# One triangle of symmetric attention scores computed, the other taken by DMA transpose, with a PSUM ring of double banks and chunked loads, in a gated attention and MLP-mixer kernel

## The chip, the cores and the metric

The kernel runs on one core of one Trainium2 chip. The metric is the device time of one execution in microseconds; the runs of a kernel are summarised by their median.

## What is computed

Eight batches of 3008 rows. `z` has 64 columns; `u` and `v` have 256. First a gated attention without softmax, then an MLP mixer over tokens and over channels, with the attention's output as its input:

```python
scores = (z @ z.T) / S                      # per batch, S = 3008: symmetric
attn = np.maximum(scores, 0.0) ** 2
x = u * (attn @ v)
# mixer
h = np.maximum(x.T @ w_tok1, 0.0) @ w_tok2  # w_tok1 3008x256, w_tok2 256x3008
u2 = x + h.T
out = u2 + np.maximum(u2 @ w_ch1, 0.0) @ w_ch2   # w_ch1 256x1536, w_ch2 1536x256
```

Inputs and output are float32; the kernel works in bf16 with float32 sums.

## The kernel before

Rows are handled in 24 tiles of 128 (the last has 64 real rows). Queries are taken in 6 blocks of 512 (the last 448 wide), keys in 6 groups of 4 tiles, so a batch has 36 groups (b, q, g): query block q against key group g. The loop runs over all 288 groups of the 8 batches.

*Attention.* `load_z` (line 67) loads z twice side by side with a casting DMA on POOL's queue, so that it fills 128 columns, and one DMA transpose on SP's queue makes `zT` (line 80): both halves of the partitions hold z transposed. `scores` (line 134) makes the scores of a group with four 64-row matmuls (line 145), two of them in the upper and two in the lower half of the rows of the array, into two PSUM tiles `sc` of two banks each; ACT applies relu and 1/S (line 151, `rl`), DVE squares (line 153, `at`). The result has keys on partitions and queries along the row. `av` (line 157) multiplies it by `v`: per key tile two matmuls of 512 columns (line 177), one for each half of v's 256 columns, both into `acc`, one PSUM tile of two banks for the whole query block. The last key tile has only 64 rows; its copy on the other 64 partitions serves the second half. After the sixth key group `gate` (line 183) multiplies `acc` by the transposed `u` (lines 191 and 196 on DVE) into `xT`, and a DMA transpose makes `x` (line 199). The `acc` tag has one buffer, so the next query block's first matmul waits for the gate. `load_uT` (line 96) loads a u block and transposes it (line 108).

*Mixer.* `mixer(b)` (line 214) returns pieces of work that are run between the attention matmuls of batch b+1: `tok1` (line 226: 8 matmuls of 256 columns into `a_ps`, over the six query blocks one sum), `tok2` (line 239: `h_ps`, added to `xT` by DVE on line 243), `ch1` (line 257: `hp`, one bank, 512 channels-by-rows per piece, relu on ACT, line 209, or DVE, line 212, whichever a running count has less loaded) and `ch2` (line 271: 24 matmuls of 256 columns into `op`; the sum with `u_sb` on DVE, line 277, and the store, line 281). All mixer tiles share the tag `mm`: two single banks. PSUM is so divided: two `sc` tiles of two banks, `acc` two banks, `mm` two banks.

*Order.* The program is emitted by hand and every engine's queue keeps that order. In group n the scores of group n+1 come first, then the four key tiles of group n, and after each of them mixer pieces as long as a budget lasts; a batch's share of mixer cost is spread evenly over the 36 groups. Each piece has an earliest group. In batch 0 no mixer work exists; after the last group the whole mixer of batch 7 is left and runs alone. At the very start (lines 312 to 316) POOL's queue gets z, v, u block 0, all weights and u block 1 of batch 0, in this order; the next batch's z is fetched at its query block 1 and its v at block 2.

Of the kernel before, what the change touches and what calls it, by code (L numbers as in the profile page):

```python
# [7 lines left out]
F32 = mybir.dt.float32  # L8
# [4 lines left out]
P = 128  # L13
QW = 512
# [13 lines left out]
def kernel(  # L28
# [38 lines left out]
    def load_z(b):  # L67


        zr = sb.tile([P, KT, 2, d_qk], BF16, tag="zr", name="zr", bufs=1)  # L70
        for h in range(2):
            nc.gpsimd.dma_start(
                out=zr[:, : KT - 1, h, :],
                in_=z[b, : (KT - 1) * P, :].rearrange("(t p) d -> p t d", p=P))
            for r in range(2):
                nc.gpsimd.dma_start(
                    out=zr[r * TAIL:(r + 1) * TAIL, KT - 1, h, :],
                    in_=z[b, (KT - 1) * P:, :])
        zT = sb.tile([P, KT, P], BF16, tag="zT", name="zT", bufs=2)
        nc.sync.dma_start_transpose(out=zT[:], in_=zr.rearrange("p t h d -> p (t h d)"))  # L80
        return zT.rearrange("p t s -> p (t s)")

    def load_v(b, parts):
        vt = sb.tile([P, KT, D], BF16, tag="v", name="v_sb", bufs=2)
        step = (KT - 1 + parts - 1) // parts
        for t0 in range(0, KT - 1, step):
            t1 = min(t0 + step, KT - 1)
            nc.gpsimd.dma_start(  # L88
                out=vt[:, t0:t1, :],
                in_=v[b, t0 * P:t1 * P, :].rearrange("(t p) d -> p t d", p=P))  # L90
        for r in range(2):
            nc.gpsimd.dma_start(
                out=vt[r * TAIL:(r + 1) * TAIL, KT - 1, :], in_=v[b, (KT - 1) * P:, :])
        return vt

    def load_uT(b, q):
        ur = sb.tile([P, QW // P, D], BF16, tag="ur", name="ur", bufs=2)
        full = widths[q] // P
        rest = widths[q] - full * P
# [11 lines left out]
        return uT  # L111
# [16 lines left out]
    zTs, vs, uTs = {}, {}, {}  # L128
    xTs, xs = {}, {}
    groups = [(b, q, g) for b in range(B) for q in range(NQ) for g in range(NG)]  # L130
    accs = {}
    attn = {}

    def scores(n):
        b, q, g = groups[n]
        zT = zTs[b]
        W = widths[q]
        tiles = []
        pss = []
        for pr in range(GK // 2):  # L140
            sc = psum.tile([P, 2, QW], F32, tag="sc", name="sc", bufs=2)
# [7 lines left out]
        for sc in pss:  # L149
            rl = sb.tile([P, 2, QW], BF16, tag="rl", name="rl", bufs=3)  # L150
            nc.scalar.activation(rl[:, :, :W], sc[:, :, :W], ACT.Relu, scale=inv_S)  # L151
            at = sb.tile([P, 2, QW], BF16, tag="at", name="at", bufs=5)
            nc.vector.tensor_mul(at[:, :, :W], rl[:, :, :W], rl[:, :, :W])  # L153
            tiles.append(at)
        attn[n] = tiles

    def av(n):

        b, q, g = groups[n]
        W = widths[q]  # L160
        if g == 0:
            accs[b, q] = psum.tile([P, DT, QW], F32, tag="acc", name="acc", bufs=1)
        acc = accs[b, q]
        tiles = attn.pop(n)
        vt = vs[b]
        order = list(range(GK))
        if g == NG - 1:
            order = [GK - 1] + order[:-1]

        def one(i, last):  # L170
            k = g * GK + i
            at = tiles[i // 2][:, i % 2, :W]
            for dh in range(DT):
                rows = slice(0, P)
                if k == KT - 1:
                    rows = slice(dh * TAIL, (dh + 1) * TAIL)
                nc.tensor.matmul(  # L177
                    acc[:, dh, :W], vt[rows, k, dh * P:(dh + 1) * P], at[rows],
                    start=(k == 0), stop=(g == NG - 1 and last), skip_group_check=True)

        return [lambda i=i, j=j: one(i, j == GK - 1) for j, i in enumerate(order)]

    def gate(b, q):
        W = widths[q]
        acc = accs.pop((b, q))
        uT = uTs.pop((b, q))
        xT = sb.tile([P, DT, QW], BF16, tag="xT", name="xT", bufs=13)
        if W < QW:
            nc.gpsimd.memset(xT[:, :, W:], 0.0)
        full, rest = W // P, W % P  # L190
        nc.vector.tensor_mul(  # L191
            xT[:, :, :full * P].rearrange("p h (t s) -> p h t s", s=P),
            acc[:, :, :full * P].rearrange("p h (t s) -> p h t s", s=P),
            uT[:, :full].rearrange("p t h s -> p h t s"))
        if rest:
            nc.vector.tensor_mul(
                xT[:, :, full * P:W], acc[:, :, full * P:W], uT[:, full, :, :rest])
        x = sb.tile([P, DT, QW // P, P], BF16, tag="x", name="x_sb", bufs=7)
        nc.sync.dma_start_transpose(
            out=x.rearrange("p h t d -> p (h t) d"), in_=xT.rearrange("p h s -> p (h s)"))  # L200
        xTs[b, q], xs[b, q] = xT, x


    load = {"ACT": 0.0, "DVE": 0.0}

    def relu_out(dst, src, n):
        if load["ACT"] + 0.1 + n / 1200 <= load["DVE"] + 0.15 + n / 960:
            load["ACT"] += 0.1 + n / 1200
            nc.scalar.activation(dst, src, ACT.Relu)  # L209
        else:  # L210
            load["DVE"] += 0.15 + n / 960
            nc.vector.tensor_single_scalar(dst, src, 0.0, AX.max)  # L212

# [174 lines left out]
```

## Time and profile before

| | |
|---|---|
| median of 3 runs | 1467.13 us (1466.74 to 1468.72) |
| the profiled execution | 1467.17 us |
| span of its profile (first to last instruction) | 1465.4 us |
| PE busy | 1296.3 us, 7488 matmuls |
| DVE / ACT busy | 700.0 / 760.6 us |
| DMA | 105.75 MB, mean 72 GB/s |

The profile takes one execution apart by engine: PE is the matrix engine (PEld its weight loads), DVE and ACT the two elementwise engines, POOL and SP the queues that here issue DMAs. A row "A <- B" under waits says that A's engine stood idle until B was done, with the total, the number of times and the longest, all in us. A row of the timeline starts with its time from the start of the span and its length. In a row of instruction groups stand the count, the busy time, the mean in ns, and the idle time before. A matmul's end is modelled, so its duration overlaps with the next one's; start-to-start distances are what counts.

### The profile page before, as it was taken

The page shows a single profiled execution, that of the slowest core. Times are in us where ns is not written, and L with a number is a line of the kernel's source. Part 1 is how long each engine was busy: PE and PEld are TensorE (multiplying, and loading weights), DVE is VectorE, ACT ScalarE, POOL GpSimd, SP SyncE. Part 2 cuts the span into 40 slices and gives each one's busy share as a digit, 9 for nine tenths or more (in the row PEclk, how much of TensorE's full clock was granted, in tenths as well). Part 3 has the DMA queues.
Part 4 walks back from the last instruction along what each step waited for, and adds up shares of the span by engine and source line. Part 5 has one row for each costly group of instructions (what it writes and reads, how often), then busy time and mean ns, then how long its engine had stood idle before and what let it go on. Part 6 is the DMA issues. An engine that isn't in the chain of part 4 may idle for free.

```text
span 1465.4 us, 18578 instructions
## 1 busy us (share of the span) xinstructions
PE 1296.3 (88%) x7488; PEld 630.6 (43%) x7488; DVE 700.0 (48%) x1028; ACT 760.6 (52%) x965; POOL 126.9 (9%) x178
## 2 busy tenths in 40 slices
PE   1998889998999889988999989989899898999987
PEld 0334344543445334443444434445344453444455
DVE  0565554454544544445444454444544445454432
ACT  1776455545655455554555445554555544555232
POOL 5221000110010100100001100011000000000000
PEclk9999999999999999999999999999999999999999
DMA  9997522663234732629225482155512223111311
GB/s 160 174 130 87 93 46 56 73 100 71 51 62 68 121 64 45 72 50 130 54 45 65 72 125 47 43 62 97 99 43 44 58 49 72 36 37 30 70 37 49
DMA packets 308070, 105.75 MB, mean 72 GB/s; under 512 B 230224, under 2 KB 307472, under 8 KB 307984
## 3 DMA queue, kind: packets, MB, share of 16 engines
q1 hardware_dynamic: 202624, 68.71, 23.0%
q0 software_dynamic: 105360, 35.86, 22.6%
q8 instruction: 58, 0.95, 0.3%
q14 instruction: 28, 0.23, 0.0%
HBM read 71.70 MB, written 24.64 MB: 66 GB/s over the span
## 4 chain that ended last, share of the span: by engine, by line
PE 60%; ACT 13%; DVE 11%; issue 10%; DMA 5%; POOL 0%; ACTq 0%; DVEq 0%; SPq 0%; POOLq 0%
PE acc L177 22%; PE op L271 18%; PE hp L257 11%; ACT rl L151 9%; PE sc L145 6%; ACT h2pre L209 4%; DVE xT L191 3%; DMA x_sb<-xT 3%; DVE at L153 3%; DVE h2pre L212 2%; DVE xT L243 2%; PE h_ps L239 2%; PE a_ps L226 1%; DMA zT<-zr 1%; DVE res L277 0%
## 5 line engine op out<-in xcount | busy, mean ns | idle before, releaser
L151 ACT ACTIVATE rl<-sc 128x1024 bf16<-128x1024 f32 (+1 forms) x576 | 547.9, 1003 | 488.6 <-PE sc L145 487.8
L177 PE MATMUL acc<-at,v_sb 128*128 128x512 bf16 (+2 forms) x2304 | 593.0, 376 | 52.5 <-DVE xT L191 38.6
L153 DVE TENSOR_TENSOR at<-rl 128x1024 bf16<-128x1024 bf16 (+1 forms) x576 | 391.6, 681 | 462.9 <-ACT rl L151 461.9
L257 PE MATMUL hp<-xT,w_ch_sb 128*128 128x512 bf16 (+1 forms) x1152 | 318.7, 374 | 56.6 <-ACT h2pre L209 40.2
L177 PEld LDWEIGHTS <-v_sb 128*128 128x128 bf16 (+1 forms) x2304 | 203.3, 97 | 337.3 <-issue 162.6
L209 ACT ACTIVATE h2pre<-hp 128x512 bf16<-128x512 f32 (+1 forms) x380 | 217.7, 592 | 155.9 <-PE hp L257 154.3
L271 PE MATMUL op<-w_ch_sb,h2pre 128*128 128x256 bf16 (+1 forms) x2304 | 267.7, 273 | 13.5 <-ACT h2pre L209 12.0
L271 PEld LDWEIGHTS <-h2pre 128*128 128x128 bf16 (+1 forms) x2304 | 225.6, 98 | 64.0 <-issue 23.6
L257 PEld LDWEIGHTS <-w_ch_sb 128*128 128x128 bf16 x1152 | 109.4, 97 | 222.6 <-issue 122.9
L145 PE MATMUL sc<-zT 64*128 64x512 bf16 (+1 forms) x1152 | 173.9, 378 | 30.1 <-DMA zT<-zr 28.8
L212 DVE TENSOR_SCALAR h2pre<-hp 128x512 bf16<-128x512 f32 (+1 forms) x196 | 132.7, 679 | 112.2 <-PE hp L257 111.5
L277 DVE TENSOR_TENSOR res<-op,u_sb 128x512 f32<-128x512 f32 x88 | 60.9, 692 | 161.6 <-PE op L271 161.6
L100 POOL DMA_DIRECT2D ur<-in_u_dram x48 | 36.6, 763 | 991.8 <-DMA uT<-ur 919.0
L145 PEld LDWEIGHTS <-zT 64*128 64x128 bf16 x1152 | 36.3, 94 | 150.4 <-issue 121.6
L243 DVE TENSOR_TENSOR xT<-xT,h_ps 128x512 bf16<-128x512 bf16 (+1 forms) x96 | 61.1, 674 | 9.2 <-PE h_ps L239 6.9
L239 PE MATMUL h_ps<-w_tok_sb,a_sb 128*128 128x512 bf16 (+1 forms) x192 | 54.1, 373 | 10.4 <-DVE xT L243 9.1
L191 DVE TENSOR_TENSOR xT<-acc,uT 128x1024 bf16<-128x1024 f32 (+1 forms) x48 | 56.5, 1176 | 7.4 <-PE acc L177 7.4
L226 PE MATMUL a_ps<-x_sb,w_tok_sb 128*128 128x256 bf16 x384 | 45.7, 272 | 2.2 <-DMA x_sb<-xT 2.1
L226 PEld LDWEIGHTS <-w_tok_sb 128*128 128x128 bf16 x384 | 37.5, 98 | 12.4 <-issue 4.1
L239 PEld LDWEIGHTS <-a_sb 128*128 128x128 bf16 x192 | 18.4, 96 | 44.1 <-issue 29.4
L88 POOL DMA_DIRECT2D v_sb<-in_v_dram x32 | 27.0, 861 | 93.2 <-PE acc L177 93.2
L232 ACT ACTIVATE a_sb<-a_ps 128x512 bf16<-128x512 f32 x8 | 4.8, 597 | 47.5 <-PE a_ps L226 47.5
(19 smaller groups left out, 74.8 us busy)
## 6 DMA issues: line engine op xcount, KB each, us to landing
out_dram<-res SPq DMA_DIRECT2D x88, 256.0 KB, 2.1
ur<-in_u_dram POOLq DMA_DIRECT2D x40, 256.0 KB, 4.2
v_sb<-in_v_dram POOLq DMA_DIRECT2D x24, 384.0 KB, 8.1
zr<-in_z_dram POOLq DMA_DIRECT2D x16, 368.0 KB, 7.0
v_sb<-in_v_dram POOLq DMA_DIRECT2D x8, 320.0 KB, 12.1
w_ch_sb<-in_moe_w_ch_dram POOLq DMA_DIRECT2D x2, 768.0 KB, 27.6
ur<-in_u_dram POOLq DMA_DIRECT2D x8, 192.0 KB, 3.6
w_tok_sb<-in_moe_w_tok_dram POOLq DMA_DIRECT2D x1, 1504.0 KB, 26.5
```

What stands on the lines that cost most here:

```text
L145: nc.tensor.matmul(sc[:, r, :W], zT[h, k * P:(k + 1) * P], zT[h, q * QW:q * QW + W], start=True, stop=True)
L151: nc.scalar.activation(rl[:, :, :W], sc[:, :, :W], ACT.Relu, scale=inv_S)
L153: nc.vector.tensor_mul(at[:, :, :W], rl[:, :, :W], rl[:, :, :W])
L177: nc.tensor.matmul(acc[:, dh, :W], vt[rows, k, dh * P:(dh + 1) * P], at[rows], start=(k == 0), stop=(g == NG - 1 and last), skip_group_che ...
L191: nc.vector.tensor_mul(xT[:, :, :full * P].rearrange("p h (t s) -> p h t s", s=P), acc[:, :, :full * P].rearrange("p h (t s) -> p h t s", ...
L209: nc.scalar.activation(dst, src, ACT.Relu)
L212: nc.vector.tensor_single_scalar(dst, src, 0.0, AX.max)
L226: nc.tensor.matmul(st["a_ps"][:, th, :], w_tok1_sb[:, k, th * P:(th + 1) * P], x[:, :, i, :], start=(k == 0 and th == 0), stop=(k == KT - ...
L239: nc.tensor.matmul(h[:, :W], st["a"][:, th, dh * P:(dh + 1) * P], w_tok2_sb[:, th, q * QW:q * QW + W], start=(th == 0), stop=(th == 1))
L243: nc.vector.tensor_add(xT[:, dh, :W], xT[:, dh, :W], h[:, :W])
L257: nc.tensor.matmul(hp[:, :W], w_ch1_sb[:, dc, cc * P:(cc + 1) * P], xTs[b, q][:, dc, :W], start=(dc == 0), stop=(dc == DT - 1))
L271: nc.tensor.matmul(op[:rows[i], i, :], h2[:, cc, c0:c0 + rows[i]], w_ch2_sb[:, cc, :], start=(cc == 0 and i == 0), stop=(cc == CHT - 1), s ...
```

## The change

*Scores.* Only groups with g >= q are computed ("direct", 21 of 36 per batch). For g > q the squares are written to `at` in blocks of 128x128, and a DMA transpose on SP's queue makes `fl` from it (16 blocks): the tile that group (q'=g, g'=q) needs later. `fl` has ten buffers, `at` three, each for a whole group. The order of key groups in a query block now mixes direct and flipped ones.

*PSUM.* One tag `ps` of three double banks serves scores and all mixer pieces; `tok2` and `ch1` make two 512-column results per tile and one DVE or ACT instruction reads both, by strict turns for `ch1`. `acc` is split in two single-bank tiles, one for each half of the columns of v; in a group all matmuls of one half come first, then the other's, and the gate runs by halves between them.

*Loads.* z and v are loaded in chunks of one key group (z through two buffers, each chunk with its own transpose), at the start and for the next batch.

*Pace.* The budget follows the estimated length of each group; mixer pieces are run between and after the two halves of a group.

```diff
-    def load_z(b):
-        zr = sb.tile([P, KT, 2, d_qk], BF16, tag="zr", name="zr", bufs=1)
+    def load_z(b, zT, c):
+        t0, t1 = c * GK, min(c * GK + GK, KT - 1)
+        zr = sb.tile([P, GK, 2, d_qk], BF16, tag="zr", name="zr", bufs=2)
...
+        nc.sync.dma_start_transpose(
+            out=zT[:, t0:t0 + GK, :], in_=zr.rearrange("p t h d -> p (t h d)"))
...
+    def load_v(b, c):
+        vt = sb.tile([P, GK, D], BF16, tag="v", name="v_sb", bufs=8)
...
+    def key_order(q):
+        direct = list(range(q, NG))
+        if q == 0:
+            return [direct[0], direct[-1]] + direct[1:-1]
+        direct = [direct[-1]] + direct[:-1]
+        flipped = list(range(q))
+        order = []
+        while direct or flipped:
+            if direct:
+                order.append(direct.pop(0))
+            if flipped:
+                order.append(flipped.pop(0))
+        return order
+
+    groups = [(b, q, g) for b in range(B) for q in range(NQ) for g in key_order(q)]
+    directs = [t for t in groups if t[2] >= t[1]]
...
-            sc = psum.tile([P, 2, QW], F32, tag="sc", name="sc", bufs=2)
+            sc = psum.tile([P, 2, QW], F32, tag="ps", name="sc", bufs=3)
...
-            at = sb.tile([P, 2, QW], BF16, tag="at", name="at", bufs=5)
-            nc.vector.tensor_mul(at[:, :, :W], rl[:, :, :W], rl[:, :, :W])
+        at = sb.tile([P, GK * QW], BF16, tag="at", name="at", bufs=3)
+        flip = g > q
...
+            if flip:
+                r4 = rl.rearrange("p i (j s) -> p j i s", s=P)
+                nc.vector.tensor_mul(a4[:, :, pair, :], r4, r4)
+            else:
+                nc.vector.tensor_mul(a3[:, pair, :W], rl[:, :, :W], rl[:, :, :W])
+        if flip:
+            attn[b, q, g] = a4.rearrange("p j i s -> p i j s")
+            fl = sb.tile([P, GK, QW], BF16, tag="fl", name="fl", bufs=10)
+            nc.sync.dma_start_transpose(
+                out=fl.rearrange("p j (i s) -> p (j i) s", s=P), in_=at[:])
+            attn[b, g, q] = fl[:, :, :]
...
-            accs[b, q] = psum.tile([P, DT, QW], F32, tag="acc", name="acc", bufs=1)
+            accs[b, q] = [
+                psum.tile([P, QW], F32, tag=f"acc{h}", name=f"acc{h}", bufs=1)
+                for h in range(DT)]
...
-    def gate(b, q):
+    def gate(b, q, dh):
...
-        def tok2(q, dh):
-            h = psum.tile([P, QW], F32, tag="mm", name="h_ps", bufs=2)
+        def tok2(q):
+            h = psum.tile([P, DT, QW], F32, tag="ps", name="h_ps", bufs=3)
...
-            nc.vector.tensor_add(xT[:, dh, :W], xT[:, dh, :W], h[:, :W])
+            nc.vector.tensor_add(xT[:, :, :W], xT[:, :, :W], h[:, :, :W])
...
-            hp = psum.tile([P, QW], F32, tag="mm", name="hp", bufs=2)
+            hp = psum.tile([P, 2, QW], F32, tag="ps", name="hp", bufs=3)
...
-            relu_out(st["h2", q][:, cc, :W], hp[:, :W], W)
+            turn[0] += 1
+            if turn[0] % 2:
+                nc.vector.tensor_single_scalar(h2[:, :, :W], hp[:, :, :W], 0.0, AX.max)
+            else:
+                nc.scalar.activation(h2[:, :, :W], hp[:, :, :W], ACT.Relu)
...
+    load_z(0, zTs[0], 0)
+    load_v(0, 0)
+    for c in vorder[1:]:
+        load_z(0, zTs[0], c)
+        load_v(0, c)
+    load_uT(0, 0)
+    load_weights()
+    load_uT(0, 1)
...
+        if not last:
+            half(0)
+            mix(n, got / 2)
+            half(1)
+            mix(n, 0.0)
+        else:
+            half(0)
+            gate(b, q, 0)
+            half(1)
+            gate(b, q, 1)
+            mix(n, 0.0)
```

What the change moves on SP's queue: its first instructions before, all of them DMA transposes (`zT` of batch 0, three u blocks, `x` of query block 0, `zT` of batch 1; the numbers tell tiles apart):

```order
L80 DMA_TRANSPOSE zT_77<-zr_70 128x24x128
L108 DMA_TRANSPOSE uT_88<-ur_86 128x8x128
L108 DMA_TRANSPOSE uT_98<-ur_96 128x8x128
L108 DMA_TRANSPOSE uT_161<-ur_159 128x8x128
L199 DMA_TRANSPOSE x_sb_253<-xT_251 128x8x128
L80 DMA_TRANSPOSE zT_262<-zr_255 128x24x128
```

The same place after it, from the fifth z chunk of batch 0 on:

```order
L82 DMA_TRANSPOSE zT_70<-zr_99 128x4x128
L82 DMA_TRANSPOSE zT_70<-zr_105 128x4x128
L108 DMA_TRANSPOSE uT_113<-ur_111 128x8x128
L108 DMA_TRANSPOSE uT_123<-ur_121 128x8x128
L182 DMA_TRANSPOSE fl_151<-at_144 128x16x128
L182 DMA_TRANSPOSE fl_176<-at_169 128x16x128
L108 DMA_TRANSPOSE uT_188<-ur_186 128x8x128
L182 DMA_TRANSPOSE fl_203<-at_196 128x16x128
L182 DMA_TRANSPOSE fl_226<-at_219 128x16x128
L182 DMA_TRANSPOSE fl_249<-at_242 128x16x128
L182 DMA_TRANSPOSE fl_272<-at_265 128x16x128
```

The first flips (`fl`) stand behind the transposes of u blocks 0 and 1 and, after two of them, u block 2; on POOL's queue the load of u block 1 (`ur_121`) still stands behind the weights.

DVE's queue at the start of the last mixer, before (`h_ps` and `hp` are single banks of PSUM):

```order
L243 TENSOR_TENSOR xT_11966<-xT_11966,h_ps_12296 128x512
L243 TENSOR_TENSOR xT_11966<-xT_11966,h_ps_12300 128x512
L243 TENSOR_TENSOR xT_12199<-xT_12199,h_ps_12306 128x448
L243 TENSOR_TENSOR xT_12199<-xT_12199,h_ps_12310 128x448
L212 TENSOR_SCALAR h2pre_12316<-hp_12333 128x512
L212 TENSOR_SCALAR h2pre_12316<-hp_12341 128x512
```

and after (double banks):

```order
L284 TENSOR_TENSOR xT_10339<-xT_10339,h_ps_10598 128x1024
L284 TENSOR_TENSOR xT_10494<-xT_10494,h_ps_10604 128x2x448
L306 TENSOR_SCALAR h2pre_10612<-hp_10613 128x1024
L306 TENSOR_SCALAR h2pre_10626<-hp_10627 128x1024
L306 TENSOR_SCALAR h2pre_10640<-hp_10641 128x1024
L327 TENSOR_TENSOR res_10679<-op_10654,u_sb_10610 128x512
```

One instruction stands where two stood; `ch1` of a block is read by three of them on DVE (and three on ACT), and `ch2`'s first sum follows.

More of the change, by code (lines that the diff above doesn't have):

```diff
@@ L75, in load_z @@
             for r in range(2):
                 nc.gpsimd.dma_start(
[L77 to L94, printed above, removed]
+                    out=zr[r * TAIL:(r + 1) * TAIL, GK - 1],
@@ new lines, in both_tails, with half @@
+        def both_tails():
+            for dh in range(DT):
+                mm(GK - 1, dh, first, False)
+        def half(dh):
+            n = GK - 1 if tail else GK
+            for i in range(n):
+                mm(i, dh, first and i == 0 and not tail, last and i == n - 1)
+        pre = [both_tails] if tail else []
+        return pre, half
+    def gate(b, q, dh):
+        W = widths[q]
+        acc = accs[b, q][dh]
+        uT = uTs[b, q]
+        if dh == 0:
+            xTs[b, q] = sb.tile([P, DT, QW], BF16, tag="xT", name="xT", bufs=9)
+            if W < QW:
+                nc.gpsimd.memset(xTs[b, q][:, :, W:], 0.0)
+        xT = xTs[b, q]
@@ L198, in gate @@
[L198 to L212, printed above, removed]
```

282 lines of the change are left out of this document (153 added, 129 removed).

## The prediction

> **What bounds the kernel now.** I began with the page's first part and the stretches of the span, to see whether one engine is full all the way.
>
> ```profile
> PE 1296.3 (88%) x7488; PEld 630.6 (43%) x7488; DVE 700.0 (48%) x1028; ACT 760.6 (52%) x965; POOL 126.9 (9%) x178
> 0.00:40.00 40.00, 10.26 (x44) 3.26 (x44) 5.22 (x8) 8.93 (x9) 19.66 (x28) 1.00 1.30 165
> 520.00:690.00 170.00, 154.10 (x901) 75.84 (x900) 83.23 (x123) 88.81 (x113) 14.68 (x21) 1.00 0.44 66
> 1365.00:1465.40 100.40, 84.53 (x520) 50.07 (x518) 34.95 (x54) 27.26 (x48) 0.00 (x0) 0.99 0.20 52
> ```
>
> The last three rows are 40 us at the start, 170 us of the middle and the last 100 us: length, then the busy time of PE, PEld, DVE, ACT and POOL, PE's clock, DMA share, GB/s. PE is the engine that matters: about nine tenths busy in the middle at full clock, while DVE and ACT are half busy and the DMA engines stand at 0.44. At the start PE works 10 of 40 us.
>
> Next, who PE waits for (total, times, longest):
>
> ```profile
> PE hp L257 <- ACT h2pre L209: 40.2, 94, 0.9
> PE acc L177 <- DVE xT L191: 38.6, 40, 1.2
> PE sc L145 <- DMA zT<-zr: 28.8, 1, 28.8
> PE op L271 <- ACT h2pre L209: 12.0, 21, 0.7
> PE hp L257 <- DVE h2pre L212: 11.6, 38, 0.4
> PE acc L177 <- DVE xT L196: 10.4, 7, 1.5
> PE h_ps L239 <- DVE xT L243: 9.1, 33, 0.5
> ```
>
> Apart from one wait for the first transposed z, all are short waits for a PSUM tile to be read: the gate after each query block, and the single banks of the mixer.
>
> Then PE's pitch, because its busy time is modelled and overlaps. Three rows of PE in batch 0, where no mixer runs, and the mean durations by form:
>
> ```profile
> 55.17 0.60 PE L145 MATMUL sc<-zT 64*128 64x512 bf16 x4
> 55.70 1.90 PE L177 MATMUL acc<-at,v_sb 128*128 128x512 bf16 x8
> 57.54 0.60 PE L145 MATMUL sc<-zT 64*128 64x512 bf16 x4
> 706.78 2.78 PE L271 MATMUL op<-w_ch_sb,h2pre 128*128 128x256 bf16 x24
> L177 PE MATMUL acc<-at,v_sb 128*128 128x512 bf16 x1840 | 489.1, 380 | 42.3 <-DVE xT L191 31.9 <-DVE xT L196 10.4
> L271 PE MATMUL op<-w_ch_sb,h2pre 128*128 128x256 bf16 x2208 | 256.3, 272 | 13.5 <-ACT h2pre L209 12.0 <-DVE h2pre L212 1.5
> ```
>
> Eight 512-column matmuls take 1.90 us with one's tail of 0.38: pitch 0.217 us, eight are 1.74. A 256-column one: (2.78 - 0.27)/23 = 0.109. A group is 57.54 - 55.17 = 2.37, so its four score matmuls cost 0.63.
>
> Last, the ends of batch 0 and batch 7, from the transposes that follow the gates:
>
> ```profile
> 124.88 1.60 SPq L199 DMA_TRANSPOSE x_sb<-xT  x1
> 1369.26 1.28 SPq L199 DMA_TRANSPOSE x_sb<-xT  x1
> ```
>
> The span is thus 124.9 (start and batch 0), 7 batches of (1369.3 - 124.9)/7 = 177.8, and a tail of 96.1 in which the last mixer runs alone. Pure pitch of one middle batch: acc 276 full-width equivalents (288, less the 448-wide block and the paired tail rows), h_ps 23.5 and hp 141, all at 0.217: 95.6; a_ps 48 and op 288 at 0.109: 36.6; 36 score bursts at 0.63: 22.7. Sum 154.9. The other 23 us per batch are the waits above, each with the 0.16 of the next matmul's start that the modelled tail hides.
>
> **The change, part by part.** *Scores.* 21 of 36 groups keep their burst: 15 x 0.63 = 9.5 us less per batch, so the pitch floor is 145.4. Relu and multiply go with them, off PE's path.
>
> *The flips.* 15 per batch, 16 blocks of 128x128 each. Rows for transposes of 8 and 24 blocks (SP's issue time min/median/max, the landing, and the 16 engines in 3.4 us around one 8-block transpose):
>
> ```profile
> L108 SPq DMA_TRANSPOSE uT<-ur x48: 1232/1282/5532, 24.1 to 1294.5; - x48
> L80 SPq DMA_TRANSPOSE zT<-zr x8: 3612/3731/9844, 10.1 to 1037.2; - x8
> uT<-ur SPq DMA_TRANSPOSE x48, 3.1
> zT<-zr SPq DMA_TRANSPOSE x8, 5.7
> q1 hardware_dynamic: 1056, 0.26, 40.0%
> ```
>
> Sixteen blocks: issue 3.73 x 16/24 = 2.5 us, landing between 3.1 and 5.7, say 4.4; DMA engines 2 x 0.40 x 3.4 = 2.7 us. Per batch that is 37 us of SP and 41 us of DMA on top of 0.44 x 170 = 75: 116 of some 155. Every flipped tile is produced at least six groups (10 us or more) before its use, so landing is hidden in the steady state. The cover is thin only in block 0 of each batch: five flips, one each 2.37 us, almost no mixer work beside them, three `at` buffers. SP needs 2.5 each. Cost 0 to 6 us per batch (the upper end if each is 1.2 us late, as an 8-block transpose has landed after up to 13.5), I take 2.
>
> ```profile
> DMA to landing us min/median/max: 3.0/3.2/13.5
> ```
>
> The Trainium skill speaks against these flips: its page "VectorE: DVE Perf Modes", section "The three transpose paths", prices one 128x128 transpose at 390 ns on TensorE and 1309 ns by DMA, and advises TensorE where the result may go to PSUM. In the rows above the 24 blocks of zT land in 5.7 us together, 0.24 us a block, so the page's figure is not one that adds up over blocks; the sum by it stands among the rivals.
>
> *The loads in chunks.* They are more DMAs on POOL's queue, which is 9% busy. A v chunk waits until PE has done with the chunk before in the last block, and is used seven groups (12 us or more) later; the nearest row, half as large again, lands in 8.1: hidden.
>
> ```profile
> v_sb<-in_v_dram POOLq DMA_DIRECT2D x24, 384.0 KB, 8.1
> ```
>
> *The flipped multiply.* It writes in runs of 128. Bounds from the nearest rows: 0.69 as the contiguous bf16 one (L153), 1.22 as a PSUM one of the same size (L191); I take 0.69, the same types and count.
>
> ```profile
> L153 DVE TENSOR_TENSOR at<-rl 128x1024 bf16<-128x1024 bf16 x480 | 331.5, 692 | 387.9 <-ACT rl L151 387.0
> L191 DVE TENSOR_TENSOR xT<-acc,uT 128x1024 bf16<-128x1024 f32 x40 | 48.8, 1221 | 5.3 <-PE acc L177 5.3
> L151 ACT ACTIVATE rl<-sc 128x1024 bf16<-128x1024 f32 x480 | 465.1, 1021 | 404.7 <-PE sc L145 404.5
> L212 DVE TENSOR_SCALAR h2pre<-hp 128x512 bf16<-128x512 f32 x165 | 113.4, 689 | 101.4 <-PE hp L257 100.9
> ```
>
> At 1.22 DVE would get 16 us more per batch, on an engine that is half idle. The same page of the Trainium skill, section "What auto-detection actually checks", asks only for 16-bit tensors of step one, by which it would stay at 0.69.
>
> *Double banks.* An hp pair is 4 x 0.217 = 0.87 us of PE; its eviction is 1.02 on ACT (L151) or 1.22 on DVE (L191's size), by turns, so each engine has 1.74. With three slots a slot is wanted two pairs, 1.74 us, after it is full, and free 1.22 and some 0.2 of signalling (an estimate) after: no wait where DVE and ACT have nothing else. In the 21 direct groups two multiplies (1.38) or two relus (2.04) stand ahead of it in their queue: 0 to 0.5 us each, 0 to 10 per batch; I take 4. The six tok2 adds are all on DVE in one burst: 6 x 1.22 = 7.3 against 5.2 of PE, 0 to 2.1; 2. The first ch2 of a block wants the last pair 10 matmuls (1.1 us) after its end, which is ready 1.2 to 1.4 after: 6 x 0.15 to 0.4, I take 1.
>
> *Gate by halves.* A half is 0.69 (512 columns from PSUM, as L212) and starts while PE does the other half (0.87); the next block's scores or mixer work cover the second. The tail rows of key block 5, first in blocks 1 to 5, want both: 0 to 0.4 six times; 1. Uncovered, the whole was 49 us in 47 waits.
>
> So a batch has 145.4 + 2 + 4 + 2 + 1 + 1 = 155.4. The bounds add to 146 and 168; a batch at either end in every term is unlikely, so 148 to 165 goes into the range. Seven: 1088.
>
> *Start and batch 0.* PE can begin as soon as one z chunk is loaded and transposed, near 9 us (issue from 1.2, and at most the 4.2 and 3.1 of a whole u block) instead of 28.8. But SP's queue is in order, and the flips stand behind the transposes of u blocks 0 and 1, whose second loads behind the weights:
>
> ```profile
> 12.13 1.50 POOL L115 DMA_DIRECT2D w_tok_sb<-in_moe_w_tok_dram  x1
> 22.61 0.76 POOL L100 DMA_DIRECT2D ur<-in_u_dram  x1
> 24.15 1.30 SPq L108 DMA_TRANSPOSE uT<-ur  x1
> 51.18 5.48 SPq L108 DMA_TRANSPOSE uT<-ur  x2
> ur<-in_u_dram POOLq DMA_DIRECT2D x40, 256.0 KB, 4.2
> ```
>
> In before that u block landed at 51.2, and nobody minded. Now PE does four groups by about 22 us and stops: the multiply of the fifth needs the `at` buffer of the first flip. The new z loads pass through two buffers, so the third to sixth each wait for a load and a transpose, some 7 us, two in flight at a time: the sixth is issued near 9 + 1.5 x 7 = 20, and the weights behind it near 23 instead of 12, while less is queued ahead of them. I put that landing at 54 (45 to 62). Then: transpose of u 1.3, first flip landed at 60, and SP is the bound until it has issued the nine flips of blocks 0 and 1 (22.5) and some 6 us of other transposes: 84, where PE stands at block 2. Remaining: 10 x 2.37 + 14 x 1.74 = 48. Batch 0 ends near 133 (122 to 145) against 124.9: the early start is worth nothing and costs 8.
>
> *Tail.*
>
> ```profile
> 1374.75 8.02 DVE L243 TENSOR_TENSOR xT<-xT,h_ps 128x512 bf16<-128x512 bf16 x12 [5.64 <-PE h_ps L239]
> 1382.22 3.75 PE L257 MATMUL hp<-xT,w_ch_sb 128*128 128x512 bf16 x12
> ```
>
> The adds shrink from 8.0 to 7.3. From 1382.2 to the end is 83.2 us, 3.7 of them after PE's last op; PE's work there is 6 x (6 x 0.87 + 48 x 0.109) = 62.7, less 0.6 for the narrow block, plus 6 x 0.3: 64 instead of 79.5. Tail 96.1 - 16 = 80 (77 to 84).
>
> *Sum.* 133 + 1088 + 80 = 1301 of span; the profiled execution was 1467.17 for a span of 1465.4, so 1.8 more: 1303. That execution is within 0.1 us of the median of the runs, 1467.13.
>
> **The rivals.** *Slower: the DMA engines become the bound.* A batch gets longer than 177.8 once a flip costs (177.8 - 75)/15 = 6.9 us of all engines. For it: while the weights load, two 8-block issues took 5.48 us, 5.5 for sixteen blocks, and the first zT 9.84, 6.6 for sixteen. Against: alone it is 2.7, and later medians are near the minima. At 8 us: 75 + 120 = 195 per batch, 145 + 7 x 195 + 80 = 1590. I give it 0.05. *Slower: blocks one after another at a fixed price.* 240 blocks per batch decide against the change from (177.8 - 75)/240 = 0.43 us a block. At the slowest issue of the rows, 5.53/8 = 0.69, a batch is 75 + 166 = 241 and the sum 145 + 7 x 241 + 82 = 1914. Against it: 0.24 a block with landing, 0.16 of issue. 0.01. By the 1309 ns of the Trainium skill's page "VectorE: DVE Perf Modes", section "The three transpose paths", it would be 75 + 314 per batch and some 2950 in all; the landing of zT disagrees.
>
> *The waits only move.* One ring for everything lets a slow read block scores and mixer alike, and the multiply that waits for a flip blocks evictions behind it on DVE. At 26 us of waits per batch, more than the 23 of before: 133 + 7 x 171.4 + 84 + 2 = 1419. For it: DVE and ACT do shared work in order; against: both half idle. 0.12 for 1380 to 1464.
>
> *Better.* Waits of 3 and batch 0 ending at 115: 115 + 7 x 148.4 + 78 + 2 = 1234. 0.07 for below 1245.
>
> *Nothing changes.* PE's queue has 14018 rows instead of 14978, 480 matmuls fewer with their weights, so the work does go; only waits that exactly replace it give no change: 0.01.
>
> **How the numbers follow.** The forecast, 0.74, gives 1303. Its bounds: 122 + 7 x 148.4 + 77 + 2 = 1240 and 145 + 7 x 165 + 84 + 2 = 1386; not all ends meet, so 1245 to 1380, which leaves out the rivals on both sides. Faster by over 0.2% (about what a measurement of this kernel can tell from no change): 0.74 + 0.12 + 0.07 = 0.93; within 0.2%: 0.01; slower: 0.06.
>
> **What would show it.** Right: PE idle from about 22 to 60 us, ended through DVE's multiply by the first flips, which stand on SP behind uT; batch 0 ends after 125; batches of 148 to 165; gate waits nearly gone; flip issue near 2.5 us. Wrong: DMA share near 1 in the middle, SP issues of 5 us there, PE waits over 20 us per batch for hp, sc or h_ps, or a PE that runs through the first 60 us.

## The result, and the profile after

The changed kernel takes 1268.69 us in the median of 4 runs (1266.92 to 1276.55), against 1466.93 us for the kernel before in 4 runs on the same chip (1465.94 to 1468.72): a ratio of 0.866, 95% interval 0.862 to 0.870. The profiled execution took 1268.15 us for a span of 1266.4. The forecast was 1303 in a range of 1245 to 1380.

The first row is the one that the prediction began with, busy time and share of the engines from the page:

```profile
PE 1185.9 (94%) x6929; PEld 623.5 (49%) x7008; DVE 578.1 (46%) x744; ACT 472.2 (37%) x489; POOL 174.7 (14%) x258
```

Then 151 us of the middle (start:end, length; busy PE, PEld, DVE, ACT, POOL; PE's clock; DMA share; GB/s):

```profile
433.00:584.00 151.00, 148.74 (x886) 79.44 (x894) 72.23 (x93) 58.77 (x61) 21.94 (x32) 1.00 0.90 139
```

PE is idle for 2.3 of 151 us there. DVE and ACT do less, and the DMA share has gone from 0.44 to 0.90. Next, who PE and the flipped multiply wait for in the whole execution (total, times, longest):

```profile
DVE at L176 <- DMA fl<-at: 57.0, 7, 39.2
PE acc L212 <- DVE at L176: 32.6, 10, 27.7
PE sc L159 <- DMA zT<-zr: 21.7, 6, 9.4
PE acc L212 <- DVE xT L238: 12.2, 20, 1.9
PE h_ps L280 <- ACT a_sb L272: 0.7, 1, 0.7
PE hp L301 <- ACT h2pre L308: 0.2, 1, 0.2
```

The mixer's waits (`hp`, `op`, `h_ps`: 73 us before) are gone, and the gate's are 12.2 instead of 49. What is left is in batch 0: the transposes of z, and the multiply (line 176) that waits for a flip to give its `at` buffer back. The last transposes of batches 0 and 7, from SP's timeline, mark their ends as before:

```profile
145.32 3.59 SPq L247 DMA_TRANSPOSE x_sb<-xT  x1
1185.84 1.23 SPq L247 DMA_TRANSPOSE x_sb<-xT  x1
```

The flip's line on SP (issue in ns, min/median/max) and its landing in us:

```profile
L182 SPq DMA_TRANSPOSE fl<-at x120: 1317/2116/6943, 59.1 to 1140.7; - x120
DMA to landing us min/median/max: 4.2/4.8/11.6
```

So the span is 145.3 + 7 x 148.6 + 80.6. Against before, batch 0 ends 20.4 us later, each of the seven batches is 29.1 shorter (-203.9 in all), and the tail is 15.5 shorter: -199.0.

The loss sits in the first 70 us. PE there, first its start and then the stop, SP's transposes, and what SP itself waited for longest in the first 150 us:

```profile
9.39 1.03 PE L159 MATMUL sc<-zT 64*128 64x512 bf16 x4 [9.39 <-DMA zT<-zr]
35.79 1.04 PE L159 MATMUL sc<-zT 64*128 64x512 bf16 x4 [5.18 <-DMA zT<-zr]
64.54 3.57 PE L212 MATMUL acc<-at,v_sb 128*128 128x512 bf16 x8 [27.71 <-DVE at L176]
30.30 28.74 SPq L108 DMA_TRANSPOSE uT<-ur  x2
59.14 4.41 SPq L182 DMA_TRANSPOSE fl<-at  x2
SPq L108 <- DMA ur<-in_u_dram: 37.8, 3, 26.2
```

PE starts at 9.4 instead of 28.8, does four groups, and stands for 27.7 us until the first flips have landed. These stood on SP behind two u transposes. The merged row from 30 to 59 is not two slow transposes: SP was done with the first by 31.6, and then stood 26.2 us for the load of u block 1. The weights were issued on POOL from 25.3 to 29.8 us and that load right behind them; the channel weights took 26.1 to land, the u block about 28.

### The profile page after: what moved, and what is told of

The parts are those of the page before. It is cut to its first block, busy times and chain, and to the rows that moved or that the text cites. A ratio compares the mean times of both kernels' runs of the same rounds, so it can differ in the third digit from the quotient of the medians.

```text
span 1266.4 us, 17085 instructions
## 1 busy us (share of the span) xinstructions
PE 1185.9 (94%) x6929; PEld 623.5 (49%) x7008; DVE 578.1 (46%) x744; ACT 472.2 (37%) x489; POOL 174.7 (14%) x258
## 4 chain that ended last, share of the span: by engine, by line
PE 80%; DMA 7%; DVE 6%; issue 3%; ACT 2%; POOL 1%; SPq 0%; DVEq 0%; ACTq 0%; POOLq 0%
PE acc L212 34%; PE op L319 20%; PE hp L301 17%; PE sc L159 5%; DMA fl<-at 4%; PE a_ps L266 3%; DVE xT L284 3%; DMA ur<-in_u_dram 2%; ACT rl L172 2%; DVE h2pre L306 1%; DVE at L176 1%; DVE xT L238 1%; DMA zr<-in_z_dram 1%; DMA zT<-zr 0%; PE h_ps L280 0%
## 5 line engine op out<-in xcount | busy, mean ns | idle before, releaser
L172 ACT ACTIVATE rl<-sc 128x1024 bf16<-128x1024 f32 x336 | 324.2, 1016 | 451.8 <-PE sc L159 422.5
L212 PE MATMUL acc<-at,v_sb 128*128 128x512 bf16 (+1 forms) x1337 | 337.5, 385 | 45.3 <-DVE at L176 32.6
L176 DVE TENSOR_TENSOR at<-rl 128x1024 bf16<-128x1024 bf16 x240 | 165.5, 692 | 271.7 <-ACT rl L172 206.6
L308 ACT ACTIVATE h2pre<-hp 128x1024 bf16<-128x1024 f32 (+1 forms) x144 | 144.9, 1006 | 281.6 <-PE hp L301 263.9
L212 PE MATMUL acc<-fl,v_sb 128*128 128x512 bf16 (+1 forms) x921 | 223.8, 370 | 2.2 <-issue 0.2
L306 DVE TENSOR_SCALAR h2pre<-hp 128x1024 bf16<-128x1024 f32 (+1 forms) x144 | 172.6, 1200 | 79.6 <-PE hp L301 79.5
L73 POOL DMA_DIRECT2D zr<-in_z_dram x96 | 72.3, 759 | 454.9 <-DMA zT<-zr 453.6
L159 PE MATMUL sc<-zT 64*128 64x512 bf16 (+1 forms) x672 | 105.4, 385 | 23.8 <-DMA zT<-zr 21.7
L178 DVE TENSOR_TENSOR at<-rl 128x1024 bf16<-128x1024 bf16 (+1 forms) x96 | 64.3, 680 | 76.5 <-ACT rl L172 71.1
L238 DVE TENSOR_TENSOR xT<-acc,uT 128x512 bf16<-128x512 f32 (+1 forms) x96 | 61.8, 665 | 71.7 <-PE acc L212 71.2
## 6 DMA issues: line engine op xcount, KB each, us to landing
w_ch_sb<-in_moe_w_ch_dram POOLq DMA_DIRECT2D x2, 768.0 KB, 26.1
```

Source lines behind the costliest of these rows:

```text
L73: nc.gpsimd.dma_start(out=zr[:, : t1 - t0, h, :], in_=z[b, t0 * P:t1 * P, :].rearrange("(t p) d -> p t d", p=P))
L159: nc.tensor.matmul(sc[:, r, :W], zT[h, k * P:(k + 1) * P], zT[h, q * QW:q * QW + W], start=True, stop=True)
L176: nc.vector.tensor_mul(a4[:, :, pair, :], r4, r4)
L212: nc.tensor.matmul(o, vt[rows, i, dh * P:(dh + 1) * P], rhs, start=st, stop=sp, skip_group_check=True)
L238: nc.vector.tensor_mul(xT[:, dh, :full * P].rearrange("p (t s) -> p t s", s=P), acc[:, :full * P].rearrange("p (t s) -> p t s", s=P), uT[: ...
L306: nc.vector.tensor_single_scalar(h2[:, :, :W], hp[:, :, :W], 0.0, AX.max)
```

## The experiments

Line numbers in the rows of an experiment are those of its own kernel. All are compared with the changed kernel (ratio 0.866 to before); "batch" is the usual distance of two batches' ends. The four runs of the changed kernel spread over 9.6 us, so a smaller difference of medians is read together with the batch ends, which come from the one profiled execution of each kernel.

| run | median, us | ratio to before (95%) | batch 0 ends | batch |
|---|---|---|---|---|
| changed kernel | 1268.69 | 0.866 (0.862 to 0.870) | 145.3 | 148.9 |
| u blocks ahead of the weights | 1279.62 | 0.871 (0.869 to 0.873) | 157.8 | 148.9 |
| weights spread over groups 8 to 22 | 1288.40 | 0.877 (0.873 to 0.882) | 162.7 | 148.9 |
| nothing flipped | 1335.84 | 0.910 (0.909 to 0.912) | 126.6 | 161.3 |
| six raw z buffers | 1282.0 | 0.873 (0.872 to 0.875) | 148.1 | 148.9 to 153.0 |
| no ring | 1375.72 | 0.937 (0.936 to 0.939) | 144.5 | 161.3 |
| gate whole | 1269.46 | 0.864 (0.863 to 0.866) | 147.4 | 148.8 |
| every flip twice | 1404.21 | 0.957 (0.954 to 0.960) | 181.1 | 160.6 to 165.3 |
| no flips in batch 0 | 1249.52 | 0.851 (0.850 to 0.852) | 126.5 | 148.9 |
| no weights | 1257.42 | 0.857 (0.856 to 0.858) | 134.2 | 148.9 |
| no flips in blocks 0, 1 of batch 0 | 1254.22 | 0.855 (0.853 to 0.856) | 130.8 | 148.9 |
| weights in group 24 | 1273.21 | 0.869 (0.867 to 0.870) | 149.4 | 148.9 |
| no flips in batch 0, weights in group 24 | 1248.76 | 0.850 (0.849 to 0.851) | 127.2 | 148.9 |

**u blocks ahead of the weights.** The prediction's cause for the stop was SP's order: flips behind the transpose of a u block whose load is behind the weights.

```diff
     load_uT(0, 0)
-    load_weights()
     load_uT(0, 1)
+    load_uT(0, 2)
+    load_weights()
```

(`ur` gets three buffers for this, and block 2 is no longer loaded later.)

> The loads of u blocks 0, 1 and 2 stand ahead of the weights (three buffers for the raw u block instead of two); nothing else moves. In-order SP theory: the first flips waited for the transposes of u blocks 1 and 2, and these for loads behind the weights. With both ahead, flips start near 35 us instead of 59, PE resumes its fifth group before 45 us instead of 64.5, and stops again when the next batch's first z chunk, behind the weights, blocks SP: 15 to 25 us less in all, 1244 to 1254 us. Rival, the DMA engines are full while the weights load, so flips that start earlier only run slower: 0 to 8 us less.

It came out 11 us slower than the changed kernel (its runs, 1274.2 to 1282.8, overlap at their lower end). SP's row in this kernel's timeline, the issue times of all its flips in ns (min/median/max), PE's resumption, and 40 to 60 us in the columns of above:

```profile
40.48 52.05 SPq L182 DMA_TRANSPOSE fl<-at  x6
L182 SPq DMA_TRANSPOSE fl<-at x120: 1317/2195/30547, 40.5 to 1155.3; - x120
79.71 3.57 PE L212 MATMUL acc<-at,v_sb 128*128 128x512 bf16 x8 [44.22 <-DVE at L176]
40.00:60.00 20.00, 0.00 (x0) 0.00 (x0) 0.00 (x0) 0.00 (x0) 1.15 (x2) 0.50 1.42 113
```

The landing of the channel weights, here first and then in the changed kernel (each load's size, then the median from issue to landing):

```profile
w_ch_sb<-in_moe_w_ch_dram POOLq DMA_DIRECT2D x2, 768.0 KB, 44.4
```

```profile
w_ch_sb<-in_moe_w_ch_dram POOLq DMA_DIRECT2D x2, 768.0 KB, 26.1
```

The u transposes were all issued by 40 us, as meant, and SP turned to the flips at once. But the first flip alone then held SP for 30.5 us and six took 52, PE stood for 44 instead of 28 us, and the weights themselves landed 18 us later; from 40 to 60 us 113 GB/s were moved, where the changed kernel moves 202. In the changed kernel SP's order does hold the flips back (the 26.2 us above), but taking it away does not help: a flip issued beside the weight loads is slow, whatever stands ahead of it. The theory that the order is worth 15 to 25 us fell.

**Weights spread, and the next batch's z later.**

```diff
-    load_weights()
...
+    for n, f in ((8, load_tok1), (14, load_tok2), (20, load_ch1), (22, load_ch2)):
+        fetch.setdefault(n, []).append(f)
...
-                fetch.setdefault(base + NG + 1 + 3 * j, []).append(
+                zn = base + NG + 1 + 3 * j if b else 3 * NG + 5 + 2 * j
+                fetch.setdefault(zn, []).append(
```

> The weights leave the start: their four loads are issued at groups 8, 14, 20 and 22 of batch 0, after u blocks 0 and 1, and batch 1's z chunks move to groups 23 to 33. In-order SP theory: nothing that SP waits for stands behind the weights any more, PE has no long stop, and batch 0 ends near 110 us instead of 144: 30 to 40 us less, 1229 to 1239 us. Rival, full DMA engines: batch 0 moves the same bytes in all, so it ends no earlier than about 130: 10 to 15 us less.

Slower by 20 us. POOL issued the weights at 39, 54 and 94 us, and SP's flips around them:

```profile
43.97 43.31 SPq L188 DMA_TRANSPOSE fl<-at  x4
90.31 20.30 SPq L188 DMA_TRANSPOSE fl<-at  x4
```

Each load of weights found flips on their way: four flips took 43 us, the next four 20. In the changed kernel, with the weights landed, four take 11:

```profile
67.46 11.41 SPq L182 DMA_TRANSPOSE fl<-at  x4
```

Spreading turned one stop into several.

**Nothing flipped.** All 36 groups compute their scores; PSUM ring, halves, chunks and pace as changed.

```diff
-    directs = [t for t in groups if t[2] >= t[1]]
+    directs = groups
...
-        flip = g > q
+        flip = False
...
-        if g >= q and ahead < len(directs):
+        if ahead < len(directs):
```

> No flips: all 36 groups compute their scores, the rest of the changed kernel stays (ring, gate by halves, chunks, order). Theory: each of the 15 groups costs 0.63 us more of PE, so a middle batch takes 148.7 + 9.5 = 158.2 us, and the start has no stop that waits for flips, so batch 0 ends near 113 instead of 144: 1268.7 + 66 - 31 = 1304 us (1295 to 1315). Rival, the flips cost the steady state as much as they save through DMA and SP: batches of 148 to 152 and about 1245 us.

The seven batches behind batch 0, of this kernel and then of the changed one, in the columns of above:

```profile
126.60:1253.00 1126.40, 1091.36 (x6433) 551.60 (x6537) 635.28 (x857) 599.21 (x634) 128.80 (x190) 1.00 0.48 75
145.30:1185.80 1040.50, 1022.24 (x6039) 542.85 (x6107) 502.14 (x645) 407.06 (x423) 128.94 (x190) 1.00 0.83 134
```

and two of this kernel's waits, over the whole execution:

```profile
PE sc L159 <- DVE h2pre L306: 10.9, 28, 0.4
PE sc L159 <- ACT h2pre L308: 1.7, 7, 0.2
```

Two results. First, 15 bursts are worth 12.4 us per batch (161.3 - 148.9), not 9.5; of the 2.9 more, 1.8 per batch (the two waits above, 12.6 us in seven batches) is `sc` waiting for the mixer's evictions in the shared ring. Second, batch 0 ends 18.7 us earlier without flips. So the flips gain 86 us in seven batches and give 19 back at the start. Per batch the DMA engines' time goes from 0.48 x 160.9 = 77 to 0.83 x 148.6 = 123 us: 3.1 for each flip. (The 151 us shown first, at 0.90, are among the fullest of the span.) The theory's sign was right, with a gain twice as large as it said (67 us, not 35).

**Six raw z buffers** instead of two, so that z's loads do not wait for its transposes.

```diff
-        zr = sb.tile([P, GK, 2, d_qk], BF16, tag="zr", name="zr", bufs=2)
+        zr = sb.tile([P, GK, 2, d_qk], BF16, tag="zr", name="zr", bufs=6)
```

> Six buffers for raw z chunks instead of two, so that no z load waits for a transpose of an earlier chunk. Theory: the weights are issued some 10 us earlier (near 14 instead of 25), u block 1 lands near 51 instead of 58, and the whole moves 5 to 9 us forward: 1260 to 1264 us. Rival, the DMA engines are busy all the time anyway and u block 1 lands when everything ahead of it has moved: no difference (under 2 us).

Neither: 13 us slower (16 in the profiled execution), 2.8 of it in batch 0, the rest as 1.5 to 4 us in five of the later batches. Over the seven later batches a flip lands after 5.3 us by the median instead of 4.7, and DVE waits 40 us in all for flips instead of 5. What the earlier z loads have to do with it was not isolated.

**No ring.** Scores back to two double banks of their own, the mixer to two single banks and single evictions.

```diff
-            sc = psum.tile([P, 2, QW], F32, tag="ps", name="sc", bufs=3)
+            sc = psum.tile([P, 2, QW], F32, tag="sc", name="sc", bufs=2)
...
-            hp = psum.tile([P, 2, QW], F32, tag="ps", name="hp", bufs=3)
-            for r in range(2):
+            for r in range(2):
+                hp = psum.tile([P, QW], F32, tag="mm", name="hp", bufs=2)
```

(and so for `a_ps`, `h_ps` and `op`)

> The ring is undone alone: scores have two double banks of their own, the mixer two single banks (tok2 and ch1 make 512 columns per tile, one eviction each, ACT and DVE by turns), as before the change; flips, gate by halves, chunks and order of the work stay. Theory: the mixer's waits come back, 78 us of idle time in the profile of before and 0.16 us hidden in each of 207 waits, 111 us less the few that the ring still has: 90 to 110 us more, 1360 to 1380 us. Rival, with 15 of 36 score groups gone ACT and DVE are so free that single banks do: under 40 us more.

+107 us, as the theory said: 12.4 per batch, 21 in the tail. The edit undoes three things together (the shared tag, the mixer's double banks, one instruction for both); what each is worth was not tested. Its waits of PE on the mixer's evictions are back:

```profile
PE hp L301 <- ACT h2pre L308: 28.1, 41, 0.7
PE hp L301 <- DVE h2pre L306: 17.5, 61, 0.4
PE h_ps L281 <- DVE xT L284: 8.6, 40, 0.3
```

**Gate whole.** One `acc` tile of two banks and one gate after both halves.

```diff
-            half(0)
-            gate(b, q, 0)
-            half(1)
-            gate(b, q, 1)
+            half(0)
+            half(1)
+            gate(b, q)
             mix(n, 0.0)
```

> The gate by halves is undone alone: acc is one tile of two banks, the gate one DVE instruction of 1024 columns after both halves. Theory: the wait of each query block comes back, about 1.2 us of 57 in all less the 15 that are left now: 30 to 45 us more, 1300 to 1313 us. Rival, the mixer work that now runs between the gate and the next block covers it in batches 1 to 7: under 12 us more.

No difference that these runs can tell; its wait for the gate:

```profile
PE acc L210 <- DVE xT L235: 16.3, 12, 3.5
```

16.3 us of waits in all instead of 12.2. The rival was right; its reading, not tested alone, is that PE has scores and mixer work to do while a whole gate runs.

**Every flip twice**, the second into a buffer that nothing reads: the price of DMA work alone, with PE's work unchanged.

```diff
             attn[b, g, q] = fl[:, :, :]
+            fl2 = sb.tile([P, GK, QW], BF16, tag="fl2", name="fl2", bufs=2)
+            nc.sync.dma_start_transpose(
+                out=fl2.rearrange("p j (i s) -> p (j i) s", s=P), in_=at[:])
```

> Each flip is done twice, the second time into a buffer that nothing reads. The changed kernel's DMA share is 0.90 in a middle batch of 149 us, 134 us of all engines. If the share is capacity, a second set of flips adds 15 x 2.7 = 41 and makes a batch 175 us: 180 to 220 us more, 1450 to 1490 us. If packets only queue and there is room, or if the flips are hidden by their long lead: under 30 us more.

Between the two: +36 us in batch 0, 12 to 16 per later batch. Its seven batches, and the first flip of each pair (issue on SP in ns, min/median/max), in batch 0 behind the weights and then in the later batches:

```profile
181.00:1322.00 1141.00, 1057.40 (x6100) 548.52 (x6099) 499.29 (x644) 406.57 (x421) 129.53 (x191) 0.96 1.03 171
L182 SPq DMA_TRANSPOSE fl<-at x13: 1602/2297/6062, 72.6 to 163.5; - x13
L182 SPq DMA_TRANSPOSE fl<-at x105: 1317/2354/7361, 184.8 to 1276.7; - x105
```

Fifteen flips more add 168 - 123 = 45 us of DMA time per batch (1.03 x 163.0 against 0.83 x 148.6; 3.0 each) and 14 us of length; batch 0 gets 36 us longer. That batch 0 lacks DMA time is not shown by this, because the second flips fill SP's queue too. By the sum of its rows SP is issuing for 112 of 116 us in batch 0, from the first flip on, and for 77% of the later batches (in the changed kernel 69 of the 72 us to 130, and 52%), and a flip of this kernel takes SP no longer in batch 0 than later. So a full queue on SP explains the 36 us as well as full DMA engines do.

**No flips in batch 0** puts the two results of the run without flips together.

```diff
+    def flips(b, q):
+        return b > 0
+
-    directs = [t for t in groups if t[2] >= t[1]]
+    directs = [t for t in groups if t[2] >= t[1] or not flips(t[0], t[2])]
...
-        flip = g > q
+        flip = g > q and flips(b, q)
...
-        if g >= q and ahead < len(directs):
+        if (g >= q or not flips(b, g)) and ahead < len(directs):
```

> The changed kernel, but batch 0 computes all 36 groups and flips none; batches 1 to 7 as changed. Theory (in batch 0 the flips share the DMA engines with the first loads and cost more than they save; later they pay): batch 0 ends at 126.6, as where nothing was flipped, instead of 145.3, and the seven batches keep 148.9: 1268.7 - 18.7 = 1250 (1244 to 1256). Rival (the stall only moves: batch 1's first flips meet the next loads and batch 1 gets the time back): batch 1 longer than 155, 1260 to 1269.

```profile
126.55 1.48 SPq L250 DMA_TRANSPOSE x_sb<-xT  x1
1166.21 1.23 SPq L250 DMA_TRANSPOSE x_sb<-xT  x1
```

1249.52 us, as forecast: 19 us faster than the changed kernel and 0.851 of before. Batch 0 ends at 126.5 and the seven batches take what they took.

**No weights.** The five loads left out, the tiles set to zero, so the mixer's result is not the reference's.

```diff
-    load_weights()
...
+    fetch.setdefault(32, []).append(set_weights)
```

> The changed kernel without the five weight loads: the four weight tiles are set to zero on POOL in group 32, so the mixer multiplies by zeros and the output is not the reference's. Theory (it is the weight loads that the first transposes and flips compete with): the stop of PE after four groups shrinks from 28 us to under 10, batch 0 ends at 105 to 120 and the time is 1228 to 1244. Rival (flips, z and u transposes fill the DMA engines by themselves, whatever else is loaded): batch 0 still ends after 135, 1258 or more.

Between the two, 1257.42 us. PE's stop on flips shrank from 27.7 to 7.2 and 3.3 us:

```profile
42.08 3.27 PE L204 MATMUL acc<-at,v_sb 128*128 128x512 bf16 x8 [7.24 <-DVE at L168]
49.21 3.57 PE L204 MATMUL acc<-at,v_sb 128*128 128x512 bf16 x8 [3.33 <-DVE at L168]
```

One of its stretches behind that:

```profile
80.00:100.00 20.00, 19.00 (x95) 6.93 (x94) 9.00 (x15) 9.81 (x11) 7.82 (x12) 1.00 1.28 169
```

The weights make most of the stop, and are worth 11 us of batch 0's end. The rest stays: without any weights batch 0 still ends 7.7 us after the kernel that flips nothing there, though PE has 15 bursts less to do. The DMA share stays above 1 until 120 us, and SP is issuing for 78 of the 93 us from 30 to 123; which of the two makes the rest was not isolated.

**No flips in query blocks 0 and 1 of batch 0**, the other six kept (`return b > 0 or q > 1` in the edit above).

> As the run without flips in batch 0, but query blocks 2 to 4 of batch 0 do flip (six of 15 flips). Theory (only flips beside the first loads cost; these come after about 65 us, when the weights have landed): six bursts less at 0.83 us, 5 us less than without any flip in batch 0: 1242 to 1250. Rival (any flip in batch 0 makes its users wait for the transfer): no gain or a loss against it, 1250 to 1262.

4.7 us slower than without any: in batch 0 even the flips behind the weights cost more than their 5 us (PE stops for 7.1 us, to 80.9, behind a multiply that waits).

**Weights in group 24**, behind nearly all flips of batch 0.

```diff
     load_uT(0, 0)
-    load_weights()
     load_uT(0, 1)
...
+    fetch.setdefault(24, []).append(load_weights)
```

> The changed kernel with the five weight loads issued in group 24 instead of in the start, near 90 us on POOL's queue, when all but the last two or three flips of batch 0 are out; the mixer first uses them near 140. Theory (batch 0 is bound by the sum of what the DMA engines are given before its last flip, and the weights are 11 us of it, as their omission showed): batch 0 ends at 134, the seven batches stay at 148.9, 1257 (1252 to 1262). Rival (the weights cost as much beside later work, as when they were spread over groups 8 to 22): batch 0 after 143, or batch 1 over 155; 1268 or more.

The rival was right: 1273.21 us, no faster than the changed kernel. POOL's first load of weights, one flip on SP, and PE:

```profile
91.84 1.50 POOL L115 DMA_DIRECT2D w_tok_sb<-in_moe_w_tok_dram  x1
96.33 1.60 SPq L108 DMA_TRANSPOSE uT<-ur  x1
98.03 24.69 SPq L182 DMA_TRANSPOSE fl<-at  x1
130.60 3.53 PE L212 MATMUL acc<-fl,v_sb 128*128 128x512 bf16 x8 [21.76 <-DMA fl<-at]
```

The early stop shrank to 8.2 us, and batch 0 lost the time again at its end: a single flip, issued 2 us behind the last weight load, took 24.7 us on SP instead of 2.1, and PE waited 21.8 for it. The u transpose ahead of it on SP took 1.6, so here no order on SP explains it: the stop goes where the weights go.

**No flips in batch 0, and the weights in group 24.**

> No flips in batch 0, and the weights issued in group 24 (near 88 us on POOL, where the DMA engines of the run without flips fall idle a little later). Theory (without the weights the u transposes of batch 0 come in time, so the 6.6 us stop at its second gate and the half clock after it go): batch 0 ends at 116 to 122 instead of 126.5, 1238 to 1246. Rival (the start is bound by z and its transposes alone, or batch 1 pays for late weights): no gain, 1247 to 1256.

The rival again: 1248.76 us is what the first edit alone gives. The second gate's stop went, but the weights beside the next batch's loads landed 42 us after issue, as its list of DMA issues has it,

```profile
w_ch_sb<-in_moe_w_ch_dram POOLq DMA_DIRECT2D x2, 768.0 KB, 42.2
```

and PE then waited for v:

```profile
118.93 2.97 PE L215 MATMUL acc<-at,v_sb 128*128 128x512 bf16 x8 [4.12 <-DMA v_sb<-in_v_dram]
```

Batch 0 ends no earlier, at 127.2.

## Why the prediction was right, and where its sizes were off

*Scores, 9.5 us per batch.* Right in kind; undoing this part alone costs 12.4 per batch with the ring in place, since `sc` then also waits for slots.

*The waits, 10 per batch (2 + 4 + 2 + 1 + 1).* The mis-sized term, and most of the miss of the total: seven batches took 1040.5 us, not 1088. The measured batch is 148.9 against the floor of 145.4, so 3.5 stand in for all five items. The 4 for `hp` and the 2 for `tok2` are near nothing (longest wait 0.2): the queueing of a multiply or relu ahead of an eviction, priced up to 0.5 a group, is not seen; that the third slot covers it is argued, not tested. The flipped multiply, on DVE, took 0.69 (mean of line 176), as chosen. The ring was underrated: taking it away costs 12.4 per batch and 21 in the tail.

*Gate by halves, 1.* The waits went as said, but the halves did not do it: the whole gate does as well.

*Where a batch's 29.1 us come from.* Undone one at a time, scores and ring are worth 12.4 each; they need not add, since the burst's 12.4 holds 1.8 of waits in the ring. The other 4.3 were not isolated; the halves are not in them. Order, pace and the chunked loads remain as candidates, not tried alone.

*Start and batch 0, 133.* 145.3 was measured, at the upper bound of its own range (122 to 145). What the prediction said would be seen was seen: four groups, a stop (from 36.8, later than the 22 forecast, since the z chunks came more slowly), an end through the flipped multiply, PE back at 64.5 (about 60 forecast). The cause that it gave is in the trace of the changed kernel: "SP's queue is in order, and the flips stand behind the transposes of u", one of which waited 26.2 us for its load behind the weights; u block 1 was there near 57.8 (54 forecast). What the prediction does not say is that the order is only half of it: with the u blocks loaded first the stop became longer, because a flip beside the weight loads itself took 30.5 us of SP. What both have in common is that the weights load at the same time; without them the stop shrank to 7.2 and 3.3. Of the 12 us that batch 0 ended late, some 4 were there when PE went on, 8 when block 2 began (92.2 for 84, with SP issuing almost without a break, at 3.1 us a flip), and the rest came behind it (53 us for 48).

*The flips' DMA time, 2.7 each.* 3.1 was measured over the seven batches, 123 us per batch in all, so the share is 0.83 (0.90 in the middle) and not the 0.75 that 116 of 155 gave; of the prediction's signs of being wrong, only this one came near. SP's issue was 2.1 by the median, for a forecast of 2.5. The rival in which the DMA engines become the bound did not come in the seven batches; how far off it was stays open, since the doubled flips load SP's queue as well. The rival of a fixed price per block did not come: sixteen blocks land in 4.8 us, 0.30 each, so the 1309 ns of the Trainium skill's page "VectorE: DVE Perf Modes", section "The three transpose paths", does not add up over the blocks of one transfer.

*Tail, 80.* 80.6. *Sum.* 12 late in batch 0, 47 early in seven batches, 1 in the tail: 1268 for 1303.

## What to carry to other kernels

A transfer that takes compute off the bounding engine is worth its price only in the stages where nothing waits for it: look there at who waits, at how full the queue is that issues it, and at the loads beside it, and keep the compute version where the transfer is late (here batch 0: 19 us). The DMA share alone does not tell: in 40 to 60 us of the kernel before it stands at 1.58, more than in any 20 us of the changed kernel's batch 0, and PE is busy for 18.7 of 20 us.

```profile
40.00:60.00 20.00, 18.66 (x96) 6.72 (x96) 11.80 (x18) 15.51 (x16) 2.58 (x3) 1.00 1.58 178
```

Order on a queue explains a late transfer, but mending the order pays only if the transfer is quick once it is issued; look at its own issue time beside other loads before moving what stands ahead of it, and move the bulk load only to a stage with nothing urgent in it. When small PSUM waits add up, a ring of more and larger slots can remove nearly all of them, as here; finer steps at the consumer then brought nothing.

## What the runs showed of the hardware

*A transpose beside bulk casting loads.* A flip takes 2.1 us of SP by the median, 24.7 behind the weight loads in group 24 and 30.5 beside them at the start, though SP and POOL are different queues. The channel weights landed after 26 us in the changed kernel, 34 in group 24 and 44 with the u blocks ahead; the 42 of group 24 without flips say that flips are not the only thing that slows them. The Trainium skill's page "DMA: Bandwidth & Descriptors", section "Rules for kernel authors", says that DMAs issued from different engines share the same 16 DMA engines and interleave; these rows agree that another queue gives no way past, and show that a transpose can lose far more than the loads beside it (in group 24 it took 12 times its median, the loads 1.3 times theirs).

*The clock after a stop.* In 40 to 60 us of the changed kernel, where PE does nothing, and after it (columns as above):

```profile
40.00:60.00 20.00, 0.00 (x0) 0.00 (x0) 0.00 (x0) 0.00 (x0) 2.24 (x3) 0.50 1.25 202
60.00:80.00 20.00, 12.04 (x39) 3.87 (x39) 6.37 (x10) 5.01 (x5) 3.46 (x5) 0.70 1.29 189
```

The granted clock falls to 0.50, and the first eight matmuls after the stop take 3.57 us instead of 1.90. The Trainium skill's page "TensorE: Matmul & The Clock Gate", part 1, says so: half rate after an idle window, full rate again after some microseconds of work. So each stop costs a little more than its length; shorter stops (7.2, 21.8 us above) show the same 3.3 to 3.6 us behind them.
